# Half-empty products of the attention output as two 64-column tiles of TensorE side by side

## The chip, the cores and the metric

The kernel runs on one core of one Trainium2 chip. The metric is the device time of one execution in microseconds (us); lower is better.

## The reference, cut to what matters

Sliding-window attention with four sink keys, followed by a feed-forward layer with a rational activation:

```python
batch, n_heads, seq, head_dim = (4, 8, 768, 64)
n_sink, window = (4, 128)

def _attn_ref(q, k, v, n_sink, window):
    scale = 1.0 / np.sqrt(D)
    scores = scale * np.matmul(q, k.transpose(0, 1, 3, 2))
    is_sink = pos[None, :] < int(n_sink)
    rel = pos[:, None] - pos[None, :]
    in_window = (rel >= 0) & (rel < int(window))
    keep = is_sink | in_window
    scores = np.where(keep, scores, -1000000000.0)
    ...                                        # softmax over the keys
    return np.matmul(a, v).astype(np.float32)

def _moe_ref(x, w_in, w_out, a, b):            # x: 3072 x 512, d_ff = 2048
    h = x @ w_in
    P = a[0] + a[1] * h + a[2] * h * h + a[3] * h * h * h
    Q = 1.0 + np.abs(b[0]) * np.abs(h) + np.abs(b[1]) * h * h
    g = P / (Q + 1e-06)
    return (g @ w_out).astype(np.float32)
```

The result may be as far from this as bf16 products put it. Only the product of the attention weights with `v` is touched by the change.

## The kernel before

The work is cut into 12 steps `s`, each of 256 query rows of one batch (three steps a batch). A step makes the attention of its rows for all 8 heads, and the feed-forward layer then takes the 256 rows. The steps overlap: TensorE goes from a piece of one step's attention to a piece of another step's layer, in a fixed order that a list (`ORDER`) gives. Heads are taken in four pairs (`i`), so that two heads of 64 fill the 128 rows of the array.

The exponentials of the scores are kept per block of 64 keys (`j`). A key with a window of 128 is seen by queries from its own block and the two blocks of 64 after it, so that a block holds 192 columns of queries. Blocks lie 256 columns apart, and the 64 columns between two blocks are zeros:

```python
EW = 256
def exps(s, i):
    e_t = e_fix[grp, s % 2]
    data = e_t[:, 64:].rearrange("p (j c) -> p j c", c=EW)[:, il * NHF:(il + 1) * NHF, 0:192]
    nc.scalar.activation(out=..., in_=ps[...], func=AF.Exp, scale=inv_sqrt_d)
```

`attend` multiplies them with `v`. A unit is 128 query rows of one pair of heads: tile `t` of the batch (0 to 5), pair `i`. The rows are two blocks of 64, numbered 2t and 2t+1, and take keys from four blocks and the sinks:

```python
def attend(s, G):
    b, g = divmod(s, GPB)
    ps = (ps_op if other else ps_mp).tile([P, 512], FP32, ..., name="ps_o")
    us = units(s, G)                              # 3 units of a step at a time (2 in the last group,
                                                  # and 2 in each of step 0's four groups)
    ps_o = ps[:, 0:len(us) * 2 * (D + 1)].rearrange("p (u c) -> p u c", u=len(us))
    for u, (n, i) in enumerate(us):
        grp, il = divmod(i, 2)
        t = g * NTS + n
        terms = []
        for j, off in ((2 * t, 0), (2 * t - 1, 64), (2 * t + 1, -64), (2 * t - 2, 128)):
            if j >= 0:
                sj = b * GPB + j // NHF
                c = 64 + EW * (il * NHF + j % NHF) + off
                terms.append((e_fix[grp, sj % 2][:, c:c + P], v_fix[sj % 3][:, i, j % NHF, :, :]))
        if t > 0:
            terms.append((e_sink[s][:, n * P:(n + 1) * P], v_sink[:, b, 2 * i:2 * i + 2, :]))
        for m, (l_, r_) in enumerate(terms):
            nc.tensor.matmul(ps_o[:, u, :], lhsT=l_, rhs=r_.rearrange("p e c -> p (e c)"),
                             start=(m == 0), stop=(m == len(terms) - 1))
```

So a unit has five products of 128 weight columns and 130 moving columns (two heads of 64 columns of `v`, and a column of ones for each, which gives the sum of the weights); a unit with `t` = 0, of which there is one tile for each batch and pair, has two. The weights of key block 2t+1 are read from 64 columns ahead of the block: the first half is zeros, and only rows 64 to 127 of the output get anything. Those of block 2t-2 are read from its column 128 on: the second half is zeros, and only rows 0 to 63 get anything. Each of these two is a half-empty product.

`normalize` on VectorE takes a group's `ps_o`: a reciprocal of the sums (line 550) and one multiplication (line 553 or 562). A group writes into one bank of PSUM, and the next group waits until that bank has been read. What else TensorE does, in the order of a step: the scores (line 476, with mask products at line 484), the sinks' scores (line 447), the first layer (line 610, 64 products of 128x256 a step) and the second layer (line 678, 32 products of 128x512 a step).

Of the kernel before, what the change touches and what calls it, by code (L numbers as in the profile page):

```python
# [72 lines left out]
def kernel(  # L73
# [13 lines left out]
    nc = tc.nc  # L87
# [6 lines left out]
    P = 128  # L94
# [6 lines left out]
    GPB = S // TS  # L101
    NSTEP = B * GPB
    NTS = TS // P
    NHF = TS // 64
    EW = 256
# [30 lines left out]
    v_fix = [t_.rearrange("p (i j e c) -> p i j e c", i=NPB, j=NHF, e=2) for t_ in v_flat]  # L136
    e_fix = {(grp, n): const_pool.tile([P, 2 * NHF * EW + 64], BF16, name=f"e_{grp}_{n}")
             for grp in range(2) for n in range(2)}
# [5 lines left out]
    v_sink = v_sink_flat.rearrange("p (b h c) -> p b h c", b=B, h=H)  # L144
# [289 lines left out]
    e_sink, ps_e, ps_a, x_n, xblk = {}, {}, {}, {}, {}  # L434
# [71 lines left out]
    def units(s, G):  # L506
        if s == 0:
            return [(n, G) for n in range(NTS)]
        every = [(n, i) for n in range(NTS) for i in range(NPB)]
        return every[3 * G:3 * G + 3]  # L510
# [4 lines left out]
    def other_bank(s, G):  # L515
        return s == 0 and G % 2 == 1

    def attend(s, G):
        b, g = divmod(s, GPB)
        other = other_bank(s, G)  # L520
        ps = (ps_op if other else ps_mp).tile([P, 512], FP32, tag="ps_out" if other else "ps_m",
                                              name="ps_o")
        us = units(s, G)
        ps_o = ps[:, 0:len(us) * 2 * (D + 1)].rearrange("p (u c) -> p u c", u=len(us))
        for u, (n, i) in enumerate(us):
            grp, il = divmod(i, 2)
            t = g * NTS + n
            terms = []
            for j, off in ((2 * t, 0), (2 * t - 1, 64), (2 * t + 1, -64), (2 * t - 2, 128)):
                if j >= 0:  # L530
                    sj = b * GPB + j // NHF
                    c = 64 + EW * (il * NHF + j % NHF) + off
                    terms.append((e_fix[grp, sj % 2][:, c:c + P], v_fix[sj % 3][:, i, j % NHF, :, :]))
            if t > 0:
                terms.append((e_sink[s][:, n * P:(n + 1) * P],
                              v_sink[:, b, 2 * i:2 * i + 2, :]))
            for m, (l_, r_) in enumerate(terms):
                nc.tensor.matmul(ps_o[:, u, :], lhsT=l_, rhs=r_.rearrange("p e c -> p (e c)"),  # L538
                                 start=(m == 0), stop=(m == len(terms) - 1))
        ps_a[s, G] = ps_o  # L540

    def normalize(s, G):
# [186 lines left out]
    for s in range(1, NSTEP):  # L729
        r_ = 4 * s - 20  # L730
# [66 lines left out]
    for i in range(NPB):  # L797
        grp, il = divmod(i, 2)
# [16 lines left out]
    for n in range(NQ0, 2 * NS_PE + 1):  # L815
        s = (n - 1) // NTS
# [4 lines left out]
    for n in range(2 * NS_PE + 1, NQT):  # L821
        s = (n - 1) // NTS
        b, T = divmod(n, S // P)
# [14 lines left out]
    for s in range(NSTEP):  # L838
        b, g = divmod(s, GPB)
# [52 lines left out]
        for G in gs:  # L892
            us = units(s, G)
            grps = sorted({i // 2 for n, i in us})
            vs_ = ([("load_v", 0, 2 * G), ("load_v", 0, 2 * G + 1)]) if s == 0 else v_loads(s)
            at = G * 4.0 / len(gs)
            bank = "ps_o" if other_bank(s, G) else "ps_m"
            piece(("attend", s, G), "PE", 0.3 * len(us), 4 * s + at - 6 + 0.8,
                  lambda s=s, G=G: attend(s, G),
                  [("mask", s, grp) for grp in grps]  # L900
                  + ([("mask", s - 1, grp) for grp in range(2)] + v_loads(s - 1)
                     if g and us[0][0] == 0 else []) + [("spread_vs",)] + ([("load_vss", h) for h in range(H)] if b else [])
                  + vs_
                  + [("sink_mask" if g == 0 else "sink_exps", s)], takes=bank)
            piece(("norm", s, G), "DVE", 0.42 + 0.137 * len(us), 4 * s + at - 5 - 0.1,
                  lambda s=s, G=G: normalize(s, G),
                  [("attend", s, G), ("scale_x",),
                   ("turned_x", s - 2) if s >= 2 else None], frees=bank)
        piece(("attended", s), "NONE", 0.0, 0, None, [("attend", s, G) for G in gs])
        for part in range(2):  # L910
            r_ = NPB * s + 2 * part + 1 - 5
# [29 lines left out]
    for m in range(NSTEP):  # L941
        r_ = 4 * m
# [10 lines left out]
        for p_ in range(np_):  # L953
            c = slice(cs[p_] * GW, cs[p_ + 1] * GW)
# [48 lines left out]
        for tt in range(NTS):  # L1003
# [10 lines left out]
            n = NTS * m + tt  # L1014
# [49 lines left out]
```

The softmax here doesn't subtract the row's maximum and nothing guards it: scores larger than these inputs give would overflow.

## Time and profile before

| | us |
|---|---|
| median of 3 runs | 254.8 |
| lowest and highest | 254.3, 254.95 |
| span of the profiled execution | 253.5 |
| TensorE busy (matmuls) | 236.2 |
| VectorE busy | 226.9 |
| ScalarE busy | 223.4 |
| GpSimd busy | 119.1 |

PE stands for TensorE's matmuls, PEld for its weight loads, DVE for VectorE, ACT for ScalarE, POOL for GpSimd, SP for the engine that issues DMAs. "L538" is line 538 of the kernel, the matmul in `attend`. A row of a group of instructions gives what is written and read, the weights' shape (rows * columns), the moving data, how many there were, busy time and the mean of one in ns, and then the idle time of the engine just before them. Matmuls overlap one another in the pipeline of the array, and the duration of one is longer than the time from its start to the start of the next; how fast TensorE goes is read from starts. Some matmul records are missing from a trace: at line 678 the page has 363 matmuls and the program 384. The granted clock of TensorE was 0.997 of full speed over the run.

### The profile page before, as it was taken

How to read it: one execution, taken by the hardware profiler on the slowest of the kernel's cores; microseconds unless marked ns; L12 is line 12 of the kernel's file. 1: busy time of each engine (PE TensorE's matmuls, PEld its weight loads, DVE VectorE, ACT ScalarE, POOL GpSimd, SP SyncE). 2: the span in 40 equal slices, each digit the busy share in tenths (PEclk: the TensorE clock that was granted, in tenths of full speed). 3: DMA queues.
4: the chain of work that ended last, by engine and by line, in shares of the span. 5: the costliest groups of instructions: out<-in, count | busy, mean ns of one | idle time of the engine just before them, and what ended most of it. 6: DMA issues, size and time to landing. Idle time of an engine off the chain costs nothing.

```text
span 253.5 us, 5171 instructions
## 1 busy us (share of the span) xinstructions
PE 236.2 (93%) x2079; PEld 176.5 (70%) x2100; DVE 226.9 (90%) x294; ACT 223.4 (88%) x209; POOL 119.1 (47%) x170
## 2 busy tenths in 40 slices
PE   8765999899999999999999999999999999998894
PEld 8664898778677759687587676786776775763341
DVE  5329299999999999999999999999999999999991
ACT  6573799989999989989998999999899998999970
POOL 7979868998984266099905609840000000000000
PEclk9999999999999999999999999999999999999998
DMA  6999999999999999999995949994205023111103
GB/s 143 154 140 151 184 142 163 174 129 129 99 131 109 95 103 178 125 132 132 134 142 66 162 47 123 144 69 106 84 2 83 0 84 84 41 44 41 41 28 139
DMA packets 107056, 27.11 MB, mean 107 GB/s; under 512 B 97816, under 2 KB 103960, under 8 KB 107032
## 3 DMA queue, kind: packets, MB, share of 16 engines
q0 software_dynamic: 75568, 13.00, 73.6%
q1 hardware_dynamic: 29936, 12.72, 26.2%
q10 hardware_dynamic: 1528, 1.06, 1.5%
q8 instruction: 16, 0.26, 0.5%
q14 instruction: 8, 0.07, 0.1%
HBM read 27.30 MB, written 6.29 MB: 133 GB/s over the span
## 4 chain that ended last, share of the span: by engine, by line
PE 50%; DVE 28%; ACT 10%; DMA 7%; issue 4%; ACTq 0%
PE ps_h L610 19%; PE ps_out L678 18%; PE ps_o L538 6%; DVE sq L648 3%; DVE num L651 3%; DVE x_n L562 3%; PE ps_s L476 3%; DMA xblk<-x_n 3%; DVE num L640 2%; DMA stage_b<-in_q_dram 2%; DVE kT L427 2%; ACT hb L617 2%; DMA stage_s<-in_v_dram 2%; DVE sq L644 2%; DVE g L664 2%
## 5 line engine op out<-in xcount | busy, mean ns | idle before, releaser
L610 PE MATMUL ps_h<-xblk,w_in_sb 128*128 128x256 bf16 x768 | 91.2, 273 | 0.3
L678 PE MATMUL ps_out<-w_out_sb,g 128*128 128x512 bf16 x348 | 84.2, 379 | 3.1 <-ACT o_t L687 2.1
L610 PEld LDWEIGHTS <-w_in_sb 128*128 128x128 bf16 x768 | 74.0, 98 | 11.4 <-DMA xblk<-x_n 0.6
L241 POOL DMA_DIRECT2D v_bd<-in_v_dram x96 | 66.2, 713 | 29.7 <-PE ps_o L538 22.8
L678 PEld LDWEIGHTS <-g 128*128 128x128 bf16 x384 | 36.9, 97 | 40.3 <-issue 2.9
L617 ACT ACTIVATE hb<-ps_h 128x1024 bf16<-128x1024 f32 x48 | 48.6, 1031 | 4.8 <-PE ps_h L610 4.2
L654 ACT ACTIVATE lnq<-den,one_eps,qsc 128x4096 f32<-128x4096 bf16 (+2 forms) x17 | 47.5, 2798 | 0.5 <-DVE den L635 0.5
L494 ACT ACTIVATE e<-ps_s 128x768 bf16<-128x768 f32 x48 | 39.3, 819 | 7.7 <-PE ps_s L484 3.6
L659 ACT ACTIVATE den<-lnq 128x4096 bf16<-128x4096 f32 (+2 forms) x17 | 44.3, 2615 | 0.1
L538 PE MATMUL ps_o<-v_bd,e 128*128 128x130 bf16 x352 | 28.8, 220 | 4.1 <-DVE kT L427 1.7
L538 PEld LDWEIGHTS <-e 128*128 128x128 bf16 x352 | 23.9, 97 | 8.6 <-DVE x_n L562 3.3
L635 DVE TENSOR_TENSOR den<-den,sq 128x4096 bf16<-128x4096 bf16 (+2 forms) x17 | 28.1, 1657 | 0.7 <-ACT sq L624 0.5
L664 DVE TENSOR_TENSOR g<-num,den 128x4096 bf16<-128x4096 bf16 (+2 forms) x17 | 28.2, 1657 | 0.5 <-ACT den L659 0.3
L648 DVE TENSOR_TENSOR sq<-sq,hb 128x4096 bf16<-128x4096 bf16 (+2 forms) x17 | 28.1, 1659 | 0.1
L651 DVE TENSOR_TENSOR num<-num,sq 128x4096 bf16<-128x4096 bf16 (+2 forms) x17 | 28.2, 1656 | 0.0
L233 POOL DMA_DIRECT2D k_bf<-in_k_dram x22 | 22.0, 999 | 13.1 <-DMA kT_flat<-k_bf 12.4
L476 PE MATMUL ps_s<-qT,kT 128*128 128x192 bf16 x192 | 26.3, 246 | 0.7 <-ACT e L494 0.7
L624 ACT ACTIVATE sq<-hb 128x2048 bf16<-128x2048 bf16 (+1 forms) x15 | 24.3, 1630 | 0.0
L225 POOL DMA_DIRECT2D q_bf<-in_q_dram x21 | 19.1, 914 | 4.2 <-issue 1.5
L476 PEld LDWEIGHTS <-kT 128*128 128x128 bf16 x192 | 16.7, 97 | 4.8 <-issue 1.1
L562 DVE SCALAR_TENSOR_TENSOR x_n<-ps_o,ratio,rec 128x384 bf16<-128x384 f32 (+1 forms) x33 | 18.9, 573 | 1.2
L644 DVE TENSOR_SCALAR sq<-sq,acoef 128x4096 bf16<-128x4096 bf16 (+2 forms) x17 | 18.2, 1071 | 0.1
(88 smaller groups left out, 238.2 us busy)
## 6 DMA issues: line engine op xcount, KB each, us to landing
out_dram<-o_t SPq DMA_DIRECT2D x22, 256.0 KB, 2.4
v_bd<-in_v_dram POOLq DMA_DIRECT2D x96, 32.0 KB, 5.0
k_bf<-in_k_dram POOLq DMA_DIRECT2D x22, 128.0 KB, 5.5
q_bf<-in_q_dram POOLq DMA_DIRECT2D x21, 128.0 KB, 5.3
w_in_sb<-in_moe_w_in_dram POOLq DMA_DIRECT2D x4, 512.0 KB, 6.9
w_out_sb<-in_moe_w_out_dram POOLq DMA_DIRECT2D x4, 512.0 KB, 6.5
stage_b<-in_q_dram ACTq DMA_DIRECT2D x2, 384.0 KB, 6.6
stage_a<-in_k_dram SPq DMA_DIRECT2D x2, 256.0 KB, 4.1
```

The source lines that it names most:

```text
L241: nc.gpsimd.dma_start(out=v_bd[s][e * 64:(e + 1) * 64, i, :, e, 0:D], in_=v[b, h, g * TS:(g + 1) * TS, :].rearrange("(j p) d -> p j d", p=64))
L476: nc.tensor.matmul(half[:, n, :], lhsT=kT_fix[s % 2][:, i * NHF + 2 * a_ + n, :], rhs=qT_fix[b % 2][:, i, c:c + 192], start=not (on_pe and ...
L494: nc.scalar.activation(out=data.rearrange("p (a n) c -> p a n c", a=2), in_=ps[:, :, 0:384].rearrange("p a (n c) -> p a n c", n=2), func=A ...
L538: nc.tensor.matmul(ps_o[:, u, :], lhsT=l_, rhs=r_.rearrange("p e c -> p (e c)"), start=(m == 0), stop=(m == len(terms) - 1))
L610: nc.tensor.matmul(ps[:, n, :], lhsT=w_in_all[:, c, fc * P:(fc + 1) * P], rhs=xblk[m][:, c, :], start=(c == 0), stop=(c == NDMC - 1))
L617: nc.scalar.activation(out=hb[m][:, j * GW:(j + 1) * GW], in_=ps_h.pop((m, j)).rearrange("p n c -> p (n c)"), func=AF.Copy)
L648: nc.vector.tensor_tensor(out=sq[m][:, c], in0=sq[m][:, c], in1=hb[m][:, c], op=ALU.mult)
L651: nc.vector.tensor_tensor(out=num[m][:, c], in0=num[m][:, c], in1=sq[m][:, c], op=ALU.add)
L654: nc.scalar.activation(out=lnq_fix[:, c], in_=den[m][:, c], func=AF.Ln, scale=qsc, bias=one_eps)
L659: nc.scalar.activation(out=den[m][:, c], in_=lnq_fix[:, c], func=AF.Exp, scale=-1.0)
L664: nc.vector.tensor_tensor(out=g_of[m][:, c], in0=num[m][:, c], in1=den[m][:, c], op=ALU.mult)
L678: nc.tensor.matmul(ps_out[m, tt], lhsT=g_of[m][:, co:co + P], rhs=w_out_all[:, fc, :], start=(fc == 0), stop=(fc == NFFC - 1))
```

## The change

The half-empty products are cut to their full half. A group first makes the full products of all its units, and then all the halves: key block 2t-2 with 64 weight columns into rows 0 to 63 of the output, key block 2t+1 with 64 weight columns into rows 64 to 127. Two halves that follow each other have different columns of the array, so that they can be in it at the same time: that is what the change is for. For `t` = 0 nothing changes but the order: block 2t+1 stays a full product, since block 2t-2 does not exist. The start flag is now set at a group's first product alone, and the stop flag at the last product of each half of the rows. No other function, no list and no buffer is changed.

```diff
         us = units(s, G)
         ps_o = ps[:, 0:len(us) * 2 * (D + 1)].rearrange("p (u c) -> p u c", u=len(us))
+        full, half = [], []
         for u, (n, i) in enumerate(us):
             grp, il = divmod(i, 2)
             t = g * NTS + n
-            terms = []
-            for j, off in ((2 * t, 0), (2 * t - 1, 64), (2 * t + 1, -64), (2 * t - 2, 128)):
-                if j >= 0:
-                    sj = b * GPB + j // NHF
-                    c = 64 + EW * (il * NHF + j % NHF) + off
-                    terms.append((e_fix[grp, sj % 2][:, c:c + P], v_fix[sj % 3][:, i, j % NHF, :, :]))
+
+            def term(j, c0, c1, part):
+                sj = b * GPB + j // NHF
+                c = 64 + EW * (il * NHF + j % NHF)
+                return (part, u, e_fix[grp, sj % 2][:, c + c0:c + c1],
+                        v_fix[sj % 3][:, i, j % NHF, :, :])
+
+            full.append(term(2 * t, 0, P, slice(0, P)))
             if t > 0:
-                terms.append((e_sink[s][:, n * P:(n + 1) * P],
-                              v_sink[:, b, 2 * i:2 * i + 2, :]))
-            for m, (l_, r_) in enumerate(terms):
-                nc.tensor.matmul(ps_o[:, u, :], lhsT=l_, rhs=r_.rearrange("p e c -> p (e c)"),
-                                 start=(m == 0), stop=(m == len(terms) - 1))
+                full.append(term(2 * t - 1, 64, 192, slice(0, P)))
+                full.append((slice(0, P), u, e_sink[s][:, n * P:(n + 1) * P],
+                             v_sink[:, b, 2 * i:2 * i + 2, :]))
+                half.append(term(2 * t - 2, 128, 192, slice(0, 64)))
+                half.append(term(2 * t + 1, 0, 64, slice(64, P)))
+            else:
+                full.append(term(2 * t + 1, -64, 64, slice(0, P)))
+        every = full + half
+        ends = {}
+        for m, (part, u, l_, r_) in enumerate(every):
+            for c in range(part.start, part.stop, 64):
+                ends[c] = m
+        ends = set(ends.values())
+
+        for m, (part, u, l_, r_) in enumerate(every):
+            nc.tensor.matmul(ps_o[part, u, :], lhsT=l_, rhs=r_.rearrange("p e c -> p (e c)"),
+                             start=(m == 0), stop=m in ends)
         ps_a[s, G] = ps_o
```

## The prediction, made before the changed kernel was run

> **What bounds the kernel now.** I read the page's first part (busy times) and fourth part (the chain that ended last), then the busy times by stretch, then the chain in order of time, then single matmuls. Busy times and chain first:
>
> ```profile
> PE 236.2 (93%) x2079; PEld 176.5 (70%) x2100; DVE 226.9 (90%) x294; ACT 223.4 (88%) x209; POOL 119.1 (47%) x170
> ...
> PE 50%; DVE 28%; ACT 10%; DMA 7%; issue 4%; ACTq 0%
> ```
>
> Three engines are nearly full, and half of the chain is TensorE. An average over the run hides stages, so I asked for stretches (busy us of each engine):
>
> ```profile
> 30.00:60.00 30.00, 28.93 (x321) 25.41 (x321) 27.64 (x45) 28.45 (x33) 25.07 (x36) 1.00 1.63 156
> 60.00:90.00 30.00, 29.06 (x264) 22.10 (x266) 29.05 (x33) 28.98 (x28) 19.36 (x25) 1.00 1.35 107
> 90.00:130.00 40.00, 39.77 (x344) 29.61 (x346) 39.46 (x41) 36.76 (x32) 26.34 (x33) 1.00 1.56 142
> 130.00:187.00 57.00, 55.68 (x498) 41.81 (x502) 56.47 (x61) 54.77 (x43) 22.79 (x30) 1.00 0.92 92
> 187.00:230.00 43.00, 42.63 (x321) 29.42 (x328) 42.72 (x34) 40.92 (x31) 0.00 (x0) 1.00 0.20 50
> ```
>
> The first number after the length is PE, the third DVE. From 30 to 230 us PE is busy 28.93 + 29.06 + 39.77 + 55.68 + 42.63 = 196.1 of 200 us. Part of that is the overhang of single matmuls, but not much room is left: TensorE is a bound nearly everywhere. From 130 to 187 DVE is as full (56.47 of 57), and there the chain runs almost wholly through DVE; elsewhere it runs mostly through PE.
>
> The change touches line 538 alone. Its rows in the list of groups:
>
> ```profile
> L538 PE MATMUL ps_o<-v_bd,e 128*128 128x130 bf16 x352 | 28.8, 220 | 4.1 <-DVE kT L427 1.7
> L538 PEld LDWEIGHTS <-e 128*128 128x128 bf16 x352 | 23.9, 97 | 8.6 <-DVE x_n L562 3.3
> ```
>
> 352 products with `v`, and 80 more with the sinks' `v`. 220 ns is the way of one matmul through the pipeline; what it costs is the time to the next start. The chain in order of time gives that (start us, us, what):
>
> ```profile
> 97.06 0.85 PE ps_o L538 x15
> 97.92 1.75 PE ps_h L610 x16
> 99.66 0.85 PE ps_o L538 x15
> ```
>
> A group of three units with 15 products takes 0.85 us, 57 ns each, and the first layer goes on at once: the same core works at full rate across the seam from one kind of work to another. So a product of `attend` holds TensorE for 57 ns, and 432 of them for 24.6 us.
>
> Last, a restart after a wait: weight loads and then matmuls around 132.19 us, where a group began after the array had been idle.
>
> ```profile
> 132.19 0.23 PEld L538 LDWEIGHTS <-e 128*128 128x128 bf16 x4 [0.37 <-DVE x_n L562]
> ```
> ```profile
> 132.19 0.40 PE L538 MATMUL ps_o<-v_bd,e 128*128 128x130 bf16 x4
> 132.43 0.22 PE L538 MATMUL ps_o<-v_sink,e_sink 128*128 128x130 bf16 x1
> ```
>
> Even with nothing loaded ahead, the first matmul starts within 10 ns of its weight load, and the first four starts take 240 ns against 4 x 57 = 228. Starting from an empty array costs about 12 ns beyond the time for which it is empty. That will matter for a drain.
>
> **What the Trainium skill says.** Four places bear on this.
> 1. "TensorEngine Tiling (Array Packing)", Key Properties: changing the tiling mode, and not just the tile, drains TensorE. No figure is given, and no run so far shows one: all matmuls of the kernel before have 128*128 weights.
> 2. The same page, Restrictions: column tiling switches off the fast weight load.
> 3. "TensorE: Matmul & The Clock Gate", LDWEIGHTS: a plain load takes P / 1.2 ns for P columns. That would be 107 ns for 128 columns; the trace shows 97 ns of duration, but a load and matmul every 57 ns, so the loads before are overlapped or quicker than that. For 64 columns the formula gives 53 ns, an estimate from that page.
> 4. The same page, Part 3: tiles in different column groups run concurrently, with about 4 ns between starts; three column tiles gave 2.38x. No trace here shows it yet.
>
> **The change part by part.**
>
> *Counting.* A unit with t > 0 has five products, one with t = 0 two. There are 12 steps x 8 units = 96 units, 16 of them with t = 0 (4 batches x 4 pairs). 80 x 5 + 16 x 2 = 432, which is 352 + 80 of the groups. Half-empty are two in each of 80 units: 160 products, which become 160 of 64 columns, in 80 pairs. The number of instructions stays the same.
>
> *What is saved.* Before: 160 x 57 ns = 9.1 us. After, if the two of a pair run side by side as in place 4: 80 x (57 + 4) = 4.9 us, saving 4.2 us. If the loads without the fast mode take turns at 53 ns each, a pair takes 107 ns: 8.6 us, saving 0.5. I take a pair at 70 ns, much nearer to the first, since loads before plainly overlap running matmuls: 5.6 us, **saving 3.5 us**.
>
> *What is added.* The full products come first in each group and the halves last, so a group that has halves goes from 128 to 64 columns once, and back once when the next work of TensorE begins (a layer, scores, or the next group's full products). Groups: 4 in step 0 (each has one unit with t = 1), 3 in each of the 8 steps in the middle or at the end of a batch, and 2 of the 3 in steps 3, 6 and 9 (their first three units all have t = 0). 4 + 24 + 6 = 34 groups, 68 changes of mode. What a drain costs is the number on which all hangs. Below, it is 0, if the mode travels with the data. Above, the new mode waits until the last matmul has left the pipeline: 220 - 57 = 163 ns of lost starts, plus the 12 ns of the restart. I take the middle, about 82, and add 12: some 90 ns. **68 x 90 ns = 6.1 us added.** This is a guess between two bounds, not a measured thing.
>
> *What moves.* The last product of a group comes with the halves, and `normalize` waits for it as before; by how much depends on the same two numbers. For a group of 15: 9 x 57 + 3 x 70 + 90 = 813 ns to its end against 855, and then 90 ns before the next work begins. DVE, ACT and the transfers get nothing to do or to save. The start flags cost nothing.
>
> *Sum on TensorE.* -3.5 + 6.1 = +2.6 us.
>
> *How much of it reaches the end.* Where PE is the bound a lost slot is never given back. PE has 200 - 196 = 4 us free from 30 to 230, in waits that a later TensorE would partly shorten, and from 130 to 187 VectorE ends most of the chain. I let 85% through: +2.2 us. **254.8 + 2.2 = 257.0 us.**
>
> **The rivals.**
>
> *A: pairs pack and the mode change is cheap.* With a change at 10 to 30 ns, 68 of them cost 0.7 to 2 us, and -4.2 + 0.7 to 2 is -2.2 to -3.5 on TensorE. From 130 to 187 us VectorE takes the gain away (it has half a us free there), and the quarter of the groups in that stretch win nothing; what comes out is some 1.5 to 2.8 us: **252 to 253.3 us**. For it: the author put all the halves at the end of a group, which keeps the changes few; the restart from an empty array costs only 12 ns. Against it: the page says drain, and the pipeline is four slots deep at this size (220 / 57).
>
> *B: full drain, no packing gain.* 68 x 175 ns = 11.9 us, less 0.5 to 4.2 us: +7.7 to +11.4 on TensorE, at 85%: **261.3 to 264.5 us**. For it: a drain to the end of the pipeline is the plain reading of the word, and the fast weight load is off. Against it: a drain may end when the array is empty, with the results still on their way to PSUM.
>
> *C: nothing arrives, since another engine is the bound.* VectorE is at 90%, ScalarE at 88%. If TensorE's waits took up either sign of the change, the time would stay at **254.3 to 255.3**. Against it: in the stretches other than 130 to 187 the chain runs from one matmul group to the next with no gap.
>
> **Range and chances.** The best conceivable case is -4.2 us, to 250.6; 2% faster would be 249.7, so that faster by over 2% needs a gain that I do not see: 0.02. 2% slower is 259.9: it needs +5.1 us at the end, so 6 us on TensorE, so a drain of 140 ns with a good pairing (68 x 0.140 = 9.5, less 3.5) or of 95 ns with none. That is a third of my range for the drain: 0.34. The rest is 0.64. For 8 in 10 I take 252.0 (rival A's good end) to 263.0 (the middle of rival B).
>
> **What would show it right or wrong.** In the changed kernel, `attend` has two groups of weights, 128 and 64 columns, and the second has 160 matmuls. The starts of the halves show the pairing: two within 10 ns and then some 50 to 60 mean that they run side by side; one every 53 to 57 means that they do not. The time from the last full start to the first half start is the drain in, from the last half start to the next work the drain out: about 150 ns each by my number (57 + 90), 60 to 90 by rival A, 230 by rival B. Step by step, 34 groups with 68 such gaps have to add up to the change of the span. The prediction is wrong if a change of mode is free or takes a full pipeline, if the halves do not pair, or if VectorE's chain has grown or shrunk by more than what TensorE handed on.

## The result and the profile after

The changed kernel takes 256.07 us, the median of 4 runs (255.95 to 256.5), against 254.88 us for the kernel before in the same comparison: a ratio of 1.0052, with a 95% interval of 1.0029 to 1.0074. That is 1.3 us more (0.7 to 1.9). Differences in us below are worked out in the same way, the ratio and its interval by the median of the kernel before in that comparison.

The page of the changed kernel, busy times and chain:

```profile
PE 239.7 (94%) x2100; PEld 173.6 (68%) x2100; DVE 228.3 (90%) x294; ACT 223.3 (88%) x209; POOL 120.3 (47%) x170
...
PE 66%; ACT 13%; DMA 11%; POOL 7%; issue 2%; DVE 0%
```

TensorE's share of the chain went from 50% to 66%, and VectorE's from 28% to nothing. The stretches, columns as before. In the changed kernel line 553 is the matmul of `attend`, 577 the multiplication of `normalize`, 625 the first layer and 693 the second; "entry" is the change to 64 columns, "exit" the change back.

```profile
60.00:90.00 30.00, 29.49 (x270) 21.92 (x269) 29.56 (x33) 28.87 (x28) 19.93 (x26) 1.00 1.22 101
90.00:130.00 40.00, 40.00 (x340) 28.71 (x339) 39.55 (x41) 37.14 (x32) 26.30 (x33) 1.00 1.53 140
130.00:187.00 57.00, 56.88 (x508) 41.48 (x506) 56.47 (x60) 54.44 (x44) 23.22 (x30) 1.00 0.98 95
187.00:230.00 43.00, 43.00 (x330) 29.05 (x329) 42.72 (x35) 40.82 (x30) 0.00 (x0) 1.00 0.19 50
```

From 90 to 130 and from 187 to 230 us TensorE now has no idle moment (40.00 of 40, 43.00 of 43), and from 130 to 187 its busy time rose from 55.68 to 56.88. So it has more to do, and it now fills most of what it had left free.

One group of three units, matmuls in order of time (start us, us):

```profile
97.87 0.28 PE L553 MATMUL ps_o<-v_bd,e 128*128 128x130 bf16 x2
97.98 0.22 PE L553 MATMUL ps_o<-v_sink,e_sink 128*128 128x130 bf16 x1
98.13 0.36 PE L553 MATMUL ps_o<-v_bd,e 128*64 128x130 bf16 x6
98.42 0.39 PE L625 MATMUL ps_h<-xblk,w_in_sb 128*128 128x256 bf16 x2
```

The last full product starts at 97.98 and the first half at 98.13, where the next full one would have started at 98.04. The starts of the six halves in the trace are 98.130, 98.133, 98.211, 98.214, 98.267 and 98.271: three pairs, 3 or 4 ns within a pair. The next layer starts at 98.423, and its second matmul 121 ns later instead of 109. From the starts of the whole trace:

| | ns | over the usual 57 |
|---|---|---|
| last full product to first half (34 times) | 147 to 150 | 91 |
| first pair to second pair | 81 | 24 |
| second pair to third | 57 | 0 |
| last half to the next work, nothing else to wait for, after two or more pairs | 150 to 153 | 95 |
| the same after a single pair | 176 to 177 | 119 to 120, the 24 are in it |
| second start after the mode changed back | 10 to 12 more than usual | 12 |

### The profile page after: what moved, and what is told of

Its sections match the earlier page's. It is cut to its first block, busy times and chain, and to the rows that moved or that the text cites. A ratio compares the mean times of both kernels' runs of the same rounds, so it can differ in the third digit from the quotient of the medians.

```text
span 254.4 us, 5193 instructions
## 1 busy us (share of the span) xinstructions
PE 239.7 (94%) x2100; PEld 173.6 (68%) x2100; DVE 228.3 (90%) x294; ACT 223.3 (88%) x209; POOL 120.3 (47%) x170
## 4 chain that ended last, share of the span: by engine, by line
PE 66%; ACT 13%; DMA 11%; POOL 7%; issue 2%; DVE 0%
PE ps_out L693 28%; PE ps_h L625 24%; PE ps_o L553 7%; DMA w_in_sb<-in_moe_w_in_dram 6%; PE ps_s L476 4%; POOL v_bd L241 3%; ACT den L674 3%; DMA v_bd<-in_v_dram 3%; ACT sq L639 2%; ACT hb L632 2%; DMA q_bf<-in_q_dram 2%; ACT e L494 2%; POOL k_bf L233 2%; ACT lnq L669 1%; PE ps_s L693 1%
## 5 line engine op out<-in xcount | busy, mean ns | idle before, releaser
L693 PE MATMUL ps_out<-w_out_sb,g 128*128 128x512 bf16 x368 | 86.5, 379 | 2.1 <-ACT o_t L702 2.1
L241 POOL DMA_DIRECT2D v_bd<-in_v_dram x96 | 65.3, 695 | 30.9 <-PE ps_o L553 23.3
L553 PE MATMUL ps_o<-v_bd,e 128*128 128x130 bf16 (+1 forms) x352 | 30.2, 224 | 1.6 <-DMA q_bf<-in_q_dram 0.7
L476 PE MATMUL ps_s<-qT,kT 128*128 128x192 bf16 x192 | 27.3, 251 | 0.6 <-ACT e L494 0.3
L553 PEld LDWEIGHTS <-e 128*128 128x128 bf16 (+1 forms) x352 | 20.7, 102 | 8.7 <-DVE x_n L577 1.7
L225 POOL DMA_DIRECT2D q_bf<-in_q_dram x21 | 20.8, 993 | 2.9 <-issue 1.3
L655 DVE TENSOR_SCALAR num<-sq,acoef 128x4096 bf16<-128x4096 bf16 (+2 forms) x17 | 18.3, 1085 | 0.1
```

The lines of the kernel that those rows point to most:

```text
L241: nc.gpsimd.dma_start(out=v_bd[s][e * 64:(e + 1) * 64, i, :, e, 0:D], in_=v[b, h, g * TS:(g + 1) * TS, :].rearrange("(j p) d -> p j d", p=64))
L476: nc.tensor.matmul(half[:, n, :], lhsT=kT_fix[s % 2][:, i * NHF + 2 * a_ + n, :], rhs=qT_fix[b % 2][:, i, c:c + 192], start=not (on_pe and ...
L553: nc.tensor.matmul(ps_o[part, u, :], lhsT=l_, rhs=r_.rearrange("p e c -> p (e c)"), start=(m == 0), stop=m in ends)
L693: nc.tensor.matmul(ps_out[m, tt], lhsT=g_of[m][:, co:co + P], rhs=w_out_all[:, fc, :], start=(fc == 0), stop=(fc == NFFC - 1))
```

## The experiments

In two columns that come back below, "on TensorE" is what a kernel adds to or takes from it by the starts of matmuls, and "at the end" is the measured difference from the kernel before.

**1. The order alone.** Full products first, half-empty ones last, one start flag for the group, but all 128 columns wide.

```diff
-                half.append(term(2 * t - 2, 128, 192, slice(0, 64)))
-                half.append(term(2 * t + 1, 0, 64, slice(64, P)))
+                half.append(term(2 * t - 2, 128, 256, slice(0, P)))
+                half.append(term(2 * t + 1, -64, 64, slice(0, P)))
```

> The order and the start flags of the change (full products of a group first, half-empty ones last, one start per group), but the half-empty products stay 128 columns wide, as before, so no change of mode. Theory M (the changes of mode cost the time): as the kernel before, within 0.4 us. Rival O (the new order or the single start flag lets the bank go later, and that costs the time): slower by the 1.2 us of the changed kernel.

Measured: 0.9968 (0.9946 to 0.9991), 0.8 us faster than before (0.2 to 1.4). The order does not cost the 1.3 us: that rival falls. The gain I had not expected either. Part of it goes with the granted clock, which differs between executions: among those with 0.997 or more (18 of 22 here, 23 of 43 of the kernel before) the medians are 254.34 and 254.74, only 0.4 us apart. In the profiles the gain lies ahead of the layers: the first layer starts at 24.8 us here (in an execution of 252.65 us, 1.75 below the median of this run), at 27.7 in the kernel before and between 26.9 and 30.1 in all other profiles, and from there to the end this kernel takes 226.1 us against 225.8. Whether the order helps the start of the kernel, or whether this is how loads happened to land, these runs do not say.

**2. Halves sorted by their columns.** First all that go to rows 0 to 63, then the others.

```diff
-        every = full + half
+        every = full + sorted(half, key=lambda h_: h_[0].start)
```

> The changed kernel with the halves of a group sorted: first all that go to rows 0 to 63, then all that go to rows 64 to 127, so that neighbours use the same columns of the array, but at the one seam. Theory M with pairing real: starts 53 to 57 ns apart instead of pairs 3 ns apart; 80 pairs less 34 seams = 46 overlaps lost at about 55 ns, 2.5 us more on TensorE than the changed kernel, of which some 40 to 90% reach the end: 1 to 2.3 us slower than the changed kernel. Rival (the pairs 3 ns apart are a matter of the records, and the array takes them one after the other): as the changed kernel, within 0.4 us.

Measured: 1.0014 (0.9989 to 1.0038), 0.4 us slower than before (-0.3 to 1.0), so not slower than the changed kernel. The main expectation failed. The matmuls of the group at the same place:

```profile
98.55 0.22 PE L553 MATMUL ps_o<-v_sink,e_sink 128*128 128x130 bf16 x1
98.69 0.37 PE L553 MATMUL ps_o<-v_bd,e 128*64 128x130 bf16 x6
99.00 0.28 PE L625 MATMUL ps_h<-xblk,w_in_sb 128*128 128x256 bf16 x1
```

Six halves in 0.37 us as before (0.36), and their starts, 98.694, 98.704, 98.775, 98.785, 98.833 and 98.842, are three pairs again, now 10 ns within a pair. Either neighbours in the program need not be in different columns, or pairs do not need two tiles at all. Run 9 tells these apart.

**3. The mode changed for each unit.** The two halves straight after their unit's full products.

```diff
-        every = full + half
+        every = []
+        for u in range(len(us)):
+            every += [x_ for x_ in full if x_[1] == u] + [x_ for x_ in half if x_[1] == u]
```

> The changed kernel with the two halves of each unit straight after its full products: 80 entries and exits instead of 34, the same products. Theory M: each entry 92 ns, exit 95 + 12 ns, first pair 24 ns, together 0.223 us; 46 more of them are 10.3 us more on TensorE than in the changed kernel; as its small slack is used up, 7 to 10 us reach the end. Rival (what slows the changed kernel is not the change of mode): within 1 us of the changed kernel.

Measured: 1.0339 (1.0291 to 1.0386), 8.7 us slower than before (7.4 to 9.9), 7.4 more than the changed kernel, inside the expected 7 to 10. There are 80 entries of 146 to 161 ns, and all but two of the 80 exits take 175 to 178. The cost goes with the number of entries and exits.

**4. Without the half-empty products.** The contributions of the two half-used key blocks are missing from the output.

```diff
-        every = full + half
+        every = full
```

> Leaves out the half-empty products altogether: the keys of one half of the window for each block of rows are missing from the output. The most that any treatment of these products could bring. TensorE is spared 160 x 57 ns = 9.1 us. Theory S (only part of what TensorE gains or loses reaches the end, as VectorE is about as full): 3 to 5 us faster than before. Rival T (TensorE is the bound nearly everywhere, 85% goes through, as predicted): 7 to 8 us faster.

Measured: 0.9875 (0.9809 to 0.9942), 3.2 us faster than before (1.5 to 4.9), of 9.1 us that TensorE is spared. This figure is not firm: it rests on two of six executions (250.73 and 253.72 us), as those more than 1.5% above the fastest are left out as slow, and the median of all six is 254.69, only 0.6 us below the kernel before. In the profile the time from the first layer's start to the end is 223.8 us, against 225.8 before. So 0.6 to 3.2 us is what leaving these products out brought, well below the 7 to 8 us of rival T. The chain and the waits for VectorE's normalisation (total us, times, longest) in this kernel, and these waits in the kernel before:

```profile
DVE 57%; ACT 15%; PE 11%; issue 9%; DMA 6%; ACTq 0%; DVEq 0%
```
```profile
PEld L553 <- DVE x_n L577: 8.0, 11, 1.3
```
```profile
PEld L538 <- DVE x_n L562: 3.3, 6, 0.7
```

VectorE takes over the chain (57%, TensorE 11%), and TensorE's weight loads wait 8.0 us for it in 11 places, where in the kernel before it was 3.3 us in 6.

**5 and 6. More work for TensorE without any change of mode.** The kernel before, with one product made three times (nine times) in each of the 34 groups. The result is the same.

```diff
+                for r_n in range(2 if m == 0 and n_full == u else 0, -1, -1):   # 8 in run 6
-                nc.tensor.matmul(ps_o[:, u, :], ..., start=(m == 0), stop=(m == len(terms) - 1))
+                    nc.tensor.matmul(ps_o[:, u, :], ..., start=(m == 0),
+                                     stop=(m == len(terms) - 1 or r_n > 0))
```

Run 5:

> The kernel before, with the first product of the first unit with five products made three times instead of once in each of 34 groups (the result is the same, each start overwrites). No change of mode: 34 x 2 x 57 ns = 3.9 us more on TensorE, about what the changed kernel adds (3.2 us by its starts). Theory S (only about 40% of such an addition reaches the end): slower than before by 1.2 to 2 us. Rival T (85% reach it): by 3.3 us.

Measured: 1.0049 (1.0025 to 1.0073), 1.2 us slower (0.6 to 1.9): theory S. A third of the 3.9 us comes through, and the chain looks like that of the changed kernel (TensorE 71%, VectorE 8%), with no product cut.

Run 6:

> As the run with two more products, but eight more in each of 34 groups: 34 x 8 x 57 ns = 15.5 us more on TensorE, no change of mode. Theory S with a slack that is used up: the first 2 to 4 us are absorbed and the rest goes through, slower by 11 to 13.5 us. If a fixed share were absorbed: 40% or 6 us. Rival T: 13.2 us or more.

Measured: 1.0454 (1.0399 to 1.0509), 11.6 us slower (10.2 to 13.0). From run 5 to run 6 TensorE gets 11.6 us more and the end moves by 10.4: once little is left of TensorE's waits for VectorE, about nine tenths go through. The line of these waits has shrunk to

```profile
PEld L540 <- DVE x_n L564: 0.5, 1, 0.5
```

**7. Halves first in the group.**

```diff
-        every = full + half
+        every = half + full
+        firsts = (0, 1) if half else (0,)
...
-                             start=(m == 0), stop=m in ends)
+                             start=m in firsts, stop=m in ends)
```

> The changed kernel with the halves ahead of the full products in each group (a start flag at the first product of each half of the rows). As many changes of mode, but the first falls between the work before (matmuls of 256 or 512 columns) and the group. Theory M: what is lost in an entry does not depend on the width of the matmul before it: 109 + 92 = 201 ns after the first layer, 216 + 92 = 308 after the second, and nothing where the group had to wait anyway; the time within 0.5 us of the changed kernel. Rival (the drain is as long as the matmul before it): entries after 512 columns lose over 200 ns, 1 us slower.

Measured: 1.0051 (1.0021 to 1.0082), 1.3 us slower than before (0.5 to 2.1), as the changed kernel. The entries take 202 or 203 ns after a matmul of 256 columns (109 otherwise), 309 or 310 after 512 (216) and 176 after 192 (82): 93 or 94 ns lost whatever the width. So the loss is a fixed time and not the length of the matmul before; what it is spent on, the traces do not show.

**8. Only the groups with three pairs.**

```diff
+            if t > 0 and not (len(us) == 3 and all(g * NTS + n_ > 0 for n_, _ in us)):
+                ...                                # all five products 128 columns wide
-            if t > 0:
+            elif t > 0:
```

> 64-column halves in the 16 groups with three pairs alone; the other 18 groups with halves stay as before. Theory M: per group 899 ns from its first start to the next work instead of 853, and 12 ns at the restart: 16 x 58 ns = 0.9 us more on TensorE than before, of which under half reaches the end: slower by 0 to 0.6 us, so still no gain. Rival (the groups with three pairs win and the small ones lose it): faster than before by 0.3 us or more.

Measured: 1.0005 (0.9977 to 1.0033), 0.1 us slower (-0.6 to 0.8). There are 16 entries of 147 to 149 ns and exits as before. No gain, as theory M has it; the rival's 0.3 us lies within the interval, so that here the starts carry the point and not the time.

**9. All halves but the last of a group into rows 0 to 63.** Half of the contributions of key block 2t+1 go to the wrong rows of the output.

```diff
-                half.append(term(2 * t + 1, 0, 64, slice(64, P)))
+                half.append(term(2 * t + 1, 0, 64, slice(64, P) if u == len(us) - 1 else slice(0, 64)))
```

> After the run with sorted halves, which still started in pairs: the changed kernel with all halves of a group sent to rows 0 to 63, but for the last one (the output is not the reference's: half of the contributions of key block 2t+1 land in the wrong rows). Theory P (two tiles are needed for two products at once, and the sorted run kept its pairs because the products of one tile overtake those of the other): starts 53 to 57 ns apart within a group, five in line in a group of three units instead of three pairs; 16 x 114 + 14 x 57 ns = 2.6 us more on TensorE than the changed kernel. Rival Q (products of 64 columns overlap whatever tile they are in): still pairs, starts as in the changed kernel.

Measured: 1.0125 (1.0088 to 1.0162), 3.2 us slower than before (2.2 to 4.1), about 1.9 more than the changed kernel. A group of three units:

```profile
97.87 0.47 PE L553 MATMUL ps_o<-v_bd,e 128*64 128x130 bf16 x6
98.27 1.92 PE L625 MATMUL ps_h<-xblk,w_in_sb 128*128 128x256 bf16 x16
```

The halves take 0.47 us instead of 0.36. Their starts are 97.868, 97.949, 97.955, 98.006, 98.065 and 98.121: the pairs are gone, and five of them stand 57 to 81 ns apart. The sixth, at 97.955, starts 6 ns after another. Which product it is can be read from the trace, where the record of a matmul also says whether it counts a semaphore up. In the 14 groups with two pairs only the product that stands last in the program does so: in the changed kernel its record starts fourth of four, 14 times of 14, and here second, 14 times of 14. In the 16 groups with three pairs, all records that count up have moved from one kernel to the other as they must if the sixth product starts third. So it is the one product for rows 64 to 127, and it has overtaken three others (two in a group of two units). The semaphore does not overtake with it: in those 14 groups it goes up 22 or 23 ns after the modelled end of the group's last matmul, 126 to 128 ns after that of the product that counts, where in the changed kernel the latter is 19 or 20 ns. With run 2 this says that two tiles are needed for two products at once, and that the order of the two tiles' products in the program matters little.

**10, 11 and 12. Stay in the mode.** If only the changes cost anything, everything can be made in 64-column products: scores, masks, sinks, both layers. L204 is the matmul in `product`, through which all of these now go.

```diff
+    two = [False]                 # True from the first product on in run 11
+    def product(out_, lhsT, rhs, start, stop):
+        for c in ((slice(0, 64), slice(64, P)) if two[0] else (slice(0, P),)):
+            nc.tensor.matmul(out_[c], lhsT=lhsT[:, c], rhs=rhs, start=start, stop=stop)
...
-                nc.tensor.matmul(ps[:, n, :], lhsT=w_in_all[:, c, fc * P:(fc + 1) * P],
+                product(ps[:, n, :], w_in_all[:, c, fc * P:(fc + 1) * P],
...                               # likewise lines 447, 476, 484, 678 and the full products of attend
     for k_, n in enumerate(ORDER):
+        two[0] = k_ > last        # run 10: after the last transpose on TensorE
```

Run 10, in which the mode changes once, at 72.7 us:

> From the last transpose on TensorE to the end (some 70 us to the end) every product is made as two of 64 columns side by side: scores, masks, sinks, both layers and the full products of attend too; before that, everything 128 wide. One change of mode instead of 68. Theory M (only the changes of mode cost; two tiles side by side are as fast as one of 128 columns): 56 pairs in that stretch spare 56 x 57 ns = 3.2 us on TensorE with nothing paid for it, of which 20 to 35% reach the end: 0.6 to 1.1 us faster than the kernel before. Rival L (twice as many instructions, and weight loads that take 106 to 110 ns instead of 97, slow the layers): the first layer's pair takes more than 109 ns and the second's more than 216; with 10% more, TensorE would lose some 13 us and the time be 10 us longer.

Measured: 0.9968 (0.9947 to 0.9989), 0.8 us faster than before (0.3 to 1.3). Rival L falls, by the starts: over the stretch from 80 us on, two products of 64 columns take 109 ns with 256 moving columns, 216 with 512, 82 with 192 and 56 with 130, the same as one of 128 columns in the kernel before. A group of three units and what follows it:

```profile
98.67 0.28 PE L204 MATMUL ps_o<-v_bd,e 128*64 128x130 bf16 x4
...
99.18 0.34 PE L567 MATMUL ps_o<-v_bd,e 128*64 128x130 bf16 x6
99.35 0.49 PE L204 MATMUL ps_h<-xblk,w_in_sb 128*64 128x256 bf16 x6
```

From 98.67 to 99.35 is 0.68 us: 12 x 57 ns, where the kernel before took 0.85 and the changed kernel 0.90. Weight loads of 64 columns do take longer:

```profile
L204 PEld LDWEIGHTS <-w_in_sb 128*64 128x64 bf16 x1152 | 62.3, 110 | 2.7 <-DMA xblk<-x_n 0.9 <-issue 0.2
...
L204 PEld LDWEIGHTS <-w_in_sb 128*128 128x128 bf16 x192 | 18.5, 98 | 2.6 <-issue 0.5
```

110 ns against 98, for half of the columns. It does not show in the starts: two such loads go with every pair, and pairs of 130 moving columns start every 56 ns, so the loads overlap with each other and with matmuls. VectorE has half of the chain (57% in the kernel without the halves):

```profile
DVE 50%; PE 36%; issue 5%; ACT 3%; DMA 3%; POOL 2%; DVEq 0%
```

Run 11:

> The same from the first product to the last, transposes included: no change of mode at all. Theory M: 80 x 57 ns = 4.6 us spared on TensorE, faster than before by 1 to 1.6 us. Rival L: as in the run from the last transpose on, and more.

Measured: 0.9988 (0.9957 to 1.002), 0.3 us faster (-1.1 to 0.5), not distinguishable from the kernel before, where 1 to 1.6 was expected. It has no change of mode and spares 80 pairs, and TensorE waits the longer for the normalisation (5.9 us in 10 places). What it lost on the run before is open.

Run 12:

> The control for the run with 64-column products from the last transpose on: the same kernel, the same order and the same mode, but the half-empty products are not cut: each is made as two of 64 columns, one of them with zero weights. Theory M (sparing the halves is what made that run 0.8 us faster than before): no gain, as the kernel before within 0.4 us, and the time from the first layer's start to the end some 1.5 us longer than in that run. Rival O (the order of the products within a group, which the run with the order alone has in common with it and which was also 0.8 us faster than before, makes the gain): faster than before by 0.8 us here too.

```diff
-                    half.append(term(2 * t - 2, 128, 192, slice(0, 64)))
-                    half.append(term(2 * t + 1, 0, 64, slice(64, P)))
+                    half.append(term(2 * t - 2, 128, 256, slice(0, P)))
+                    half.append(term(2 * t + 1, -64, 64, slice(0, P)))
```

Measured: 0.9973 (0.9948 to 0.9999), 0.7 us faster than before (0 to 1.3), which is what rival O expects and theory M does not, and too near to run 10 to tell them apart by time. The group of three units takes 0.85 us again:

```profile
98.81 0.30 PE L204 MATMUL ps_o<-v_bd,e 128*64 128x130 bf16 x4
...
99.32 0.53 PE L204 MATMUL ps_o<-v_bd,e 128*64 128x130 bf16 x12
99.66 1.93 PE L204 MATMUL ps_h<-xblk,w_in_sb 128*64 128x256 bf16 x32
```

and from the first layer's start to the end its profile has 226.5 us, against 224.3 in run 10 and 225.8 in the kernel before. In the profiles, then, cutting the halves is worth some 2 us from there on (theory M had 1.5), one execution each; in the times the lead of run 10 over its control is not shown. Runs 1 and 12 share the new order and leave TensorE as much to do as before, and both came out 0.7 to 0.8 us ahead. At a granted clock of 0.997 or more they are 0.4 and 0.3 us ahead (254.28 against 254.57 for run 12, 13 executions each), and run 10 is 0.9 (253.63 against 254.57, 18 and 26), which leans to the halves without settling it. Run 10 is faster than both given kernels; how much of that is the halves and how much the order stays open.

## Why the prediction was right

It said 257.0 us, 252.0 to 263.0, and the time is 256.07. Step by step:

**The count** (160 halves, 80 pairs, 34 groups, 68 changes of mode) is what the trace has. So are the two gaps for which the prediction named 150 ns: 147 to 150 on the way in and 150 to 153 on the way out.

**What is added.** The guess of 90 ns for a change was the middle of two bounds, and it measured 91 on the way in and 95 + 12 on the way out: 34 x 198 = 6.7 us, where the text had 6.1. Run 7 shows what the middle stands for: a fixed 92 or so ns, neither nothing nor the whole 163. That it lies near the middle was luck: the text had no ground for the middle. Rival B, a full drain, is out, and so is the cheap change of rival A.

**What is saved.** The text took a pair at 70 ns and 3.5 us. Pairs do run at 57, but the first of each group pays 24 ns more. The sum over the groups is 16 x 58 + 11 x 112 + 3 x 114 + 4 x 173 ns (groups with 15, 10, 12 and 7 products, from the first start to the next work and its restart) = 3.2 us more on TensorE, so that 6.7 - 3.2 = 3.5 us was saved. That the sum fits was luck between two errors, a pair too dear and no extra for the first.

**The sum on TensorE**: +2.6 predicted, +3.2 measured.

**How much reaches the end** is the term that was mis-sized: 85% was assumed, and 1.3 of 3.2 us is about 40%. A sign of being wrong that the prediction named came true here: VectorE's share of the chain shrank from 28% to nothing, by far more than TensorE handed on. Nor do the gaps add up to the change of the span, as it asked: they come to 3.2 us on TensorE. The text had read 4 us of free time on TensorE and called them not much; they are as large as the whole effect. The waits for the normalisation that fill them, in the weight loads of the kernel before:

```profile
150.76 0.23 PEld L538 LDWEIGHTS <-e 128*128 128x128 bf16 x4 [0.66 <-DVE x_n L562]
...
166.91 0.34 PEld L538 LDWEIGHTS <-e 128*128 128x128 bf16 x6 [0.70 <-DVE x_n L562]
...
186.91 0.23 PEld L538 LDWEIGHTS <-e 128*128 128x128 bf16 x4 [0.56 <-DVE x_n L562]
```

and the same places in the changed kernel:

```profile
133.03 0.11 PEld L553 LDWEIGHTS <-e 128*128 128x128 bf16 x2 [0.18 <-DVE x_n L577]
...
151.30 0.22 PEld L553 LDWEIGHTS <-e 128*128 128x128 bf16 x2 [0.21 <-DVE x_n L577]
...
167.53 0.34 PEld L553 LDWEIGHTS <-e 128*128 128x128 bf16 x6 [0.31 <-DVE x_n L577]
...
187.54 0.11 PEld L553 LDWEIGHTS <-e 128*128 128x128 bf16 x2
```

With the 0.37 us at 132.19 that the prediction shows, these four waits came to 2.29 us and now come to 0.70, the last being too short to be marked. Of the two others of this kind before, one (0.35 us at 163.89) is gone and one (0.67 at 49.54) has grown to 0.99. All together, 3.3 us in 6 places have become

```profile
PEld L553 <- DVE x_n L577: 1.7, 4, 1.0
```

TensorE arrives later at points where it would have waited for VectorE: about 1.6 of the 3.2 us disappear there. All runs together, sorted by what TensorE got to do; the last column but one is the time from the first layer's start to the end, against the kernel before (225.8 us), from one profile each:

| run | on TensorE, us | at the end, us | first layer to end, us | chain: TensorE, VectorE |
|---|---|---|---|---|
| 4, no halves | -9.1 | -3.2 (not firm) | -2.0 | 11%, 57% |
| 11, 64 columns throughout | -4.6 | -0.3 | -0.9 | 20%, 56% |
| 10, 64 columns late | -3.2 | -0.8 | -1.5 | 36%, 50% |
| before | 0 | 0 | 0 | 50%, 28% |
| 1, order alone | 0 | -0.8 | +0.3 | 46%, 21% |
| 12, as 10, not cut | 0 | -0.7 | +0.7 | 35%, 28% |
| 8, three pairs only | +0.9 | +0.1 | +0.2 | 30%, 54% |
| the change | +3.2 | +1.3 | +0.6 | 66%, 0% |
| 2, sorted | +3.2 | +0.4 | +0.1 | 69%, 8% |
| 7, halves first | +3.2 | +1.3 | +0.8 | 69%, 9% |
| 5, two more | +3.9 | +1.2 | +1.2 | 71%, 8% |
| 9, one tile | +5.8 | +3.2 | +2.5 | 70%, 8% |
| 3, per unit | +13.5 | +8.7 | +9.2 | 83%, 3% |
| 6, eight more | +15.5 | +11.6 | +10.9 | 79%, 8% |

The second column of run 9 is worked out (3.2 + 2.6), those of runs 10 and 11 too (56 and 80 pairs of 57 ns), that of run 8 (16 x 58 ns), that of run 3 from 80 units at 169 ns (454 ns from one unit's first start to the next unit's, against 5 x 57); runs 2 and 7 are put down with the changed kernel's. Of 3 to 4 us more on TensorE, 0.4 to 1.3 us come out, an eighth to two fifths; of 13 to 16 us, two thirds to three quarters. For what TensorE gains, the times settle less, since runs 1 and 12 spare it nothing and are as far ahead as run 10; the profiles have 0.9 to 2.0 us for 3.2 to 9.1, so that there too less than half comes out. The chain's shares move with TensorE's work, but loosely: VectorE has 21% in run 1 and 54% in run 8, two lines apart in the table. The new order is in the changed kernel too; if it brought the 0.8 us of run 1 there, the changes of mode would cost 2.1 us and not 1.3. Its profile does not show that gain (the first layer starts at 28.0 us, at 27.7 in the kernel before), and run 5, in the old order, gives a third too.

That is what two engines look like that are both almost full and wait for each other by turns: rival C was right about the mechanism, though not in full, and rival A that VectorE would take away part of a gain.

## What to carry to other kernels

Column tiles do run two 64-column products in the time of one, but a change of mode and back costs some 0.2 us of TensorE (91 + 24 + 95 + 12 = 222 ns here), so a group would have to have about four pairs of 130 columns (222 / 57, an estimate; no run has four) to break even, and three were a loss on TensorE. If the products can be had in one mode throughout, no change is paid for, though run 11, which did that, came out only 0.3 us ahead, within the noise. Before sizing a gain or loss on the busiest engine, add up its own waits for the next busiest one: with 3 to 4 us of them, as here, a loss of that size came out at two fifths or less. Adding a known number of repeated products to such a kernel measures this share directly.

## What the runs showed that was not expected

- Products of one column tile overtake those of the other: sorted by tile, they still start in pairs (10 ns instead of 3), and the pairing is lost only where all but one go to the same tile (mostly 57 to 81 ns apart). In run 9 the last product in the program overtakes up to three, while its semaphore goes up only after the group's last matmul (by 22 or 23 ns in the groups with two pairs).
- A kernel whose TensorE work is all in 64-column halves, with twice the instructions there, runs its matmuls at the same rate as in full width: 109 and 216 ns for two with 256 and 512 moving columns.
- An entry into the 64-column mode costs the same 91 to 94 ns whether the matmul before it had 130, 192, 256 or 512 moving columns.
- The start of the first layer varies between profiles from 24.8 to 30.1 us, more than most of the differences measured here; from there to the end, the kernels that give TensorE the same work are within 0.7 us of each other.
